# Half of a Fourier mix by a second level of Strassen's products: seven products of quarters over the hidden dimension, with the operands' split forms kept in DRAM

## The chip, the cores and the metric

The kernel runs on one core of a Trainium2 chip. The metric is the device time of one execution in microseconds. Several executions of the kernel before were timed, and one more was profiled; all numbers of a trace come from that one.

## The reference, cut to what matters

Two blocks are computed from the same `x` (2048 rows by 576 columns, float32) and mixed by a gate of one number per row:

```python
g = sigmoid((x * gate_w).sum(-1, keepdims=True))
a = linear_attention(x, wqkv, wo)            # 32 heads of 18, phi(t) = elu(t) + 1 + 1e-6
re = einsum("bsd,ed->bse", x, dft_hid_re)    # over the hidden dimension D = 576
im = einsum("bsd,ed->bse", x, dft_hid_im)
b = einsum("ts,bse->bte", dft_seq_re, re) - einsum("ts,bse->bte", dft_seq_im, im)   # over S = 2048
out = g * a + (1 - g) * b
```

The DFT matrices are ordinary inputs; the kernel multiplies by them as by any matrix.

## The kernel before, in words

Precision comes from splitting: each float32 operand is held as a rounded part ("hi", type fp32r, written by ScalarE in `hi_of`, L112) and a remainder ("lo", hi subtracted by VectorE in `lo_of`, L115). A product is hi·hi + hi·lo + lo·hi, three matmuls for each 128 rows of the contraction. Over D = 576 = 4·128 + 64 that is 4·3 + 2 = 14 matmuls for a result tile of 128 rows and 288 columns (half of the output's columns): the last 64 rows of hi and lo share one block of 128 rows. `steps` lists these 14, `run` (L123) issues them.

The program goes through seven stages, and TensorE's instructions stand in this order:

1. K: 16 tiles of 128 rows of `x` times `wk`, features by ScalarE and VectorE (`k_half`).
2. G: `x` transposed times K's features (L408), then the products with `wv` and `wo` that make a 576x576 matrix M per head group.
3. Q and M: 16 tiles of `x` times `wq` (`q_tile`), their normalisation on VectorE (`normalise`), a transpose on TensorE (`transposed`, L719) and the product with M. Row tile `i` of the result stands in SBUF as `acc[i]`.
4. First "pairs" stage (`pairs`): the hidden product with `dft_hid_re`. It goes over 8 pairs of row tiles (p and p + 8), each pair 2 tiles by 2 halves of 14 matmuls, 56 in all; from the four results `columns` and `rest` make seven combinations of 128x288, split in hi and lo (tile `f`).
5. First "sequence" stage (`sequence`, L663): the product with `dft_seq_re` as seven products of quarters (Winograd's form of Strassen's scheme), 8 groups j of 4 batches of 42 matmuls. `Matrix` loads the batches (`craw`, 512 KB each), VectorE adds, ScalarE and VectorE split. At a group's end VectorE adds seven banks of PSUM to four quarters and mixes them into `acc` by the gate (L679).
6. and 7. The same two stages with `dft_hid_im` and `dft_seq_im`; the last mix goes to the output.

The `x` tiles of the pairs stages are loaded from DRAM raw (`xraw`, 320 KB, L174) and split anew in each of the two stages, and `wr`/`wi` likewise (`Wide`, L225, L226). SBUF is laid out by hand: seven slots of 7168 bytes a partition serve the batches, and `LAY_R`/`LAY_I` say which places in them serve `x` tiles in the pairs stages. Queue SP issues nearly all DMAs; its order is written order up to the end of stage 3 (`manual_schedule`), and a planner's from there on. VectorE's, ScalarE's and TensorE's order is the planner's everywhere: it orders by simulated times when the program is built. GpSimd (POOL) does a few constants at the start.

Of the kernel before, what the change touches and what calls it, by code (L numbers as in the profile page):

```python
# [26 lines left out]
EPS = 1e-6  # L27

# [19 lines left out]
class Ring:  # L48
# [5 lines left out]
    def next(self):  # L54
# [18 lines left out]
LAY_R = dict(xs=(-256, 4864, 15744), hi=(20864, 9984), lo=(26624, 31232),  # L73
             low=(5, 3, 2, 1), high=(6, 0, 4))
LAY_I = dict(xs=(35840, 40960, 20096), hi=(25216, 14336), lo=(31232, 46080),
             low=(0, 4, 2, 3), high=(1, 5, 6))
# [3 lines left out]
def kernel(  # L80
# [7 lines left out]
    wo: bass.AP,  # L88
    wr: bass.AP,
    wi: bass.AP,  # L90
    cr: bass.AP,
# [14 lines left out]
    psum = ctx.enter_context(tc.tile_pool(name="psum", bufs=8, space=bass.MemoryType.PSUM))  # L106

# [5 lines left out]

    def lo_of(dst, src, hi):
        nc.vector.tensor_tensor(out=dst, in0=src, in1=hi, op=ALU.subtract)  # L115

    def add(dst, a, b, op=ALU.add):
        nc.vector.tensor_tensor(out=dst, in0=a, in1=b, op=op)  # L118

# [9 lines left out]
    in_order = ExitStack()  # L129
    in_order.enter_context(tc.manual_schedule(engines={mybir.EngineType.SP}))  # L130
# [46 lines left out]
    def split_next():  # L177
# [27 lines left out]
    class Wide:  # L205
# [22 lines left out]
        def split(self, h, n=1, keep=lambda ins: ins):  # L228
# [11 lines left out]
            keep(hi_of(hi[:, KC], rest))  # L240
# [19 lines left out]

    K_AT = T_AT + NT * XD
    pk = [at(T_AT + s * XD, [P, 2, D], R, "pk") for s in range(NT)]
    x_at(LAY_Q)
    wkt = Wide(wk, dict(hi=(0, WH), lo=(2 * WH, 2 * WH + WL)), K_AT)

    def k_half(i, h, xs):
        ps = bank()[:, :HALF]
        run(ps, steps(xs, lambda j: wkt.row(h, j)))
        feature(acc[i][:, half(h)], ps)
        if h == 1:  # L270
            hi_of(pk[i][:, 0], acc[i], EPS)
            nc.vector.scalar_tensor_tensor(pk[i][:, 1], acc[i], EPS, pk[i][:, 0],
                                           op0=ALU.add, op1=ALU.subtract)
# [32 lines left out]
    for h in range(2):  # L306
        for i in range(2):
            k_half(i, h, xs[i])
            if h == 1:
                load_next()  # L310
                if i == 0:
                    split_next()
# [17 lines left out]
    def xg_next():  # L330
        if xg_raw:
            c, t, raw = xg_raw.pop(0)
            hi_of(t[:, 0], raw)
# [5 lines left out]

    for i in range(2, NT):  # L340
        xs = split.pop(0)
        split_next()
        for h in range(2):
            k_half(i, h, xs)
        if i == NT - 2:
            for _ in range(4):
                xg_load()
        load_next()
    xg_next()
    xg_next()  # L350


    wqt = Wide(wq, LAY_Q, widths=QH)
    wq_splits = (s for h in range(2) for s in wqt.split(h, 2))
# [15 lines left out]
    def load_pair(o, src, n=P):  # L370
# [4 lines left out]
        hi_of(t[:n, 0], raw[:n])  # L375
        lo_of(t[:n, 1], raw[:n], t[:n, 0])
        return t
# [19 lines left out]
    wvt[0] = load_pair(wv_ring.next(), wv[:, 0])  # L397
    step = 0
    for c in range(5):
        ps = [bank(), bank()]  # L400
        passes = FULL if c < KC else FULL[:2]
        for q in range(NCU):
            t = xg_split.pop(0)
            for k in range(CU):
                s = q * CU + k
                for n, (a, b) in enumerate(passes):
                    for h in range(2):
                        nc.tensor.matmul(ps[h][:, :HALF], t[:, a, k], pk[s][:, b, half(h)],  # L408
                                         start=(s == 0 and n == 0),
                                         stop=(s == NT - 1 and n == len(passes) - 1))  # L410
            xg_load()
            xg_next()
            if q == 1 and c:
                kv_step(c - 1)
            if q == 2 and c < 4:
                wvt[c + 1] = load_pair(wv_ring.next(), wv[:, c + 1])
# [4 lines left out]
            elif step == NT - 1:  # L421
                z_chain()
            else:
                g = step - NT
                wot.append(load_pair(wo_at[g], wo[g * GW:g * GW + gsize(g)], gsize(g)))
            if step in (4, 5):
                wqt.load(step - 4)
            if step >= 8:
# [3 lines left out]
        for h in range(2):  # L432
            hi_of(gt[:, 0, half(h)], ps[h][:, :HALF])
            lo_of(gt[:, 1, half(h)], ps[h][:, :HALF], gt[:, 0, half(h)])
    split_next()
    wot.append(load_pair(wo_at[4], wo[4 * GW:], gsize(4)))


    def q_tile(i):
# [6 lines left out]
        nc.scalar.activation(g, ps[:, HALF:HALF + 1], AF.Exp, scale=-1.0)  # L446
# [69 lines left out]
    def split_m():  # L516
        for h in range(2):
            tc.keep_in_program_order(hi_of(mhi[:, :KC, half(h)], mraw[:, :, half(h)]))
# [7 lines left out]
    LEAD = 10  # L526
    q_tile(0)
# [5 lines left out]
    for i in range(3, LEAD):  # L533
# [3 lines left out]
        if i in (4, 6, 8):  # L537
            normalise(i // 2 - 2)
# [4 lines left out]
    factors = []  # L543

    def pairs(wd, m):


        def product(b, i, h, xs):
            run(b[i][h], steps(xs[i], lambda j: wd.row(h, j)))

        def banks():
            b12, b11, b22, b21 = (bank()[:, :HALF] for _ in range(4))
            return (b11, b12), (b21, b22)

        def columns(p, b):

            t = at(T_AT + p * TPAIR, [P, 2, 7, HALF], R, "f")
            for i in range(2):
                hi_of(t[:, 0, i], b[i][0])
                lo_of(t[:, 1, i], b[i][0], t[:, 0, i])  # L560
            return t

        def rest(b, t):
            (b11, b12), (b21, b22) = b
            s = at(Y_AT, [P, 4, HALF], F, "tsum")
            nc.scalar.activation(s[:, 3], b12, AF.Copy)
            add(s[:, 0], s[:, 3], b11, ALU.subtract)
            add(s[:, 2], b22, s[:, 3], ALU.subtract)
            hi_of(t[:, 0, 2], b22)
            add(s[:, 1], b22, s[:, 0], ALU.subtract)  # L570
            add(s[:, 3], s[:, 1], b21, ALU.subtract)
            lo_of(t[:, 1, 2], b22, t[:, 0, 2])
            hi_of(t[:, 0, 3:7], s)
            lo_of(t[:, 1, 3:7], s, t[:, 0, 3:7])
            factors.append(t)

        for p in range(NP - 2):
            xs = [split.pop(0), split.pop(0)]
            b = banks()
            for i, h in sorted(((0, 0), (0, 1), (1, 0), (1, 1)), key=lambda u: u[not p]):  # L580
                product(b, i, h, xs)
                if h == 1:
                    load_next()
                    split_next()
            rest(b, columns(p, b))
            if p == NP - 4:
                m.load(0)
                m.make(0)
        xs_ring.at, xs_ring.n = [T_AT + NP * TPAIR - XS], 0
        load_next()  # L590
        split_next()
        last, p = [], NP - 2
        for k in range(2):
            xs, b = [split.pop(0), split.pop(0)], banks()
            for i in (0, 1) if k == 0 else (1, 0):
                product(b, i, 0, xs)
            if k == 0:
                split_next()
            last.append((b, xs, columns(p + k, b)))
        m.load(1)  # L600
        for b, xs, t in last:
            for i in range(2):
                product(b, i, 1, xs)
            if t is last[0][2]:
                m.make(1)
            rest(b, t)


    class Matrix:


        def __init__(self, src, lay):
# [3 lines left out]
            self.low, self.high = Ring(0, 0, 0), Ring(0, 0, 0)  # L616
            self.low.at = [SLOT_AT + k * SLOT for k in lay["low"]]
            self.high.at = [SLOT_AT + k * SLOT for k in lay["high"]]

        def load(self, upto):  # L620
            while self.todo and self.loaded <= upto:
                j, b = self.todo.pop(0)
                o = self.low.next()
# [5 lines left out]
        def make(self, upto):  # L629
            while self.raws and self.made <= upto:  # L630
                r, o = self.raws.pop(0)
                add(r[:, 0:2], r[:, 4:6], r[:, 3].unsqueeze(1).to_broadcast([P, 2, BS, P]))
                add(r[:, 2], r[:, 1], r[:, 4])
                add(r[:, 3], r[:, 2], r[:, 6])
                hi = at(self.high.next(), [P, 7, BS, P], R, "c")
                lo = at(o, [P, 7, BS, P], R, "c")
                hi_of(hi, r)
                lo_of(lo, r, hi)
                self.ready.append((hi, lo))
                self.made += 1  # L640


    PRODUCTS = {1: (4, 0), 6: (2, 4), 2: (6, 1), 5: (1, 3), 7: (0, 5), 3: (3, 2), 4: (5, 6)}

    def sequence(m, g, last=None, between=None):
        late, held = [], []
        for n in range(NP * NB):
            j, b = divmod(n, NB)
            if b == 0:
                ps = {k: bank()[:, :HALF] for k in PRODUCTS}  # L650
            c = m.ready.pop(0)
            m.load(n + 3)
            m.make(n + 2)
# [4 lines left out]
            for q, (l, f) in PRODUCTS.items():  # L658
                for b, c in held:
                    for k in range(BS):  # L660
                        p = b * BS + k
                        for i, (x, y) in enumerate(FULL):
                            nc.tensor.matmul(ps[q], c[x][:, l, k], factors[p][:, y, f],  # L663
# [9 lines left out]
            y = at(Y_AT, [P, 2, 2, HALF], F, "y")  # L673
            c11, c12, c21, c22 = (y[:, i // 2, i % 2] for i in range(4))

            def mix(t, v, h=None, g=g, out=out if last is not None else None):
                a, cs = acc[t], slice(0, D) if h is None else half(h)
                a = a[:, cs]
                nc.vector.scalar_tensor_tensor(a, v, g[:, t:t + 1], a, op0=ALU.mult, op1=ALU.add)  # L679
                if out is not None:  # L680
                    nc.sync.dma_start(out=out[t * P:(t + 1) * P, cs], in_=a)
# [3 lines left out]
            add(c11, ps[2], c11)  # L685
            if end:
# [5 lines left out]
                mix(j + NP, c21, 0, out=None)  # L692
                mix(j, c12, 1, last, out=None)
                mix(j, ps[3], 1)
                mix(j + NP, ps[4], 0, last)
            else:
# [5 lines left out]
                late += [lambda t=t, i=i, y=y: mix(t, y[:, i].rearrange("p a b -> p (a b)"))  # L702
# [139 lines left out]
```

## Time and profile before

| | |
|---|---|
| time, median of 3 runs | 745.35 us (744.57 to 745.51) |
| the profiled execution: its own time, its span | 745.01 us, 743.3 us |
| TensorE busy | 735.4 us (99%), 5540 matmuls |
| VectorE busy, ScalarE busy | 543.2 us (73%), 331.9 us (45%) |
| GpSimd busy | 1.6 us |
| granted TensorE clock | full speed in all 40 slices |
| DMA | 75.55 MB, mean 102 GB/s |

The span is the profiled part of the execution; 1.7 us of the execution's time lie around it. "Busy" of TensorE counts pipelined matmuls end to end, so 99% says that matmuls followed each other without a gap, and not that the array did all it could. The DMA share in the views below is the mean busy share of the core's 16 DMA engines.

### The profile page before, as it was taken

Reading aid. Unit: us, or ns where it says so; the run is one execution under the profiler, and the core shown is the slowest. Engines: PE = TensorE matmul, PEld = TensorE weight load, DVE = VectorE, ACT = ScalarE, POOL = GpSimd, SP = SyncE. Lnnn points to the kernel's source line nnn. Section 1 sums busy time; section 2 is a strip of 40 time slices with the busy share of each in tenths; the row PEclk is TensorE's granted clock in tenths of the full one; section 3 lists DMA queues with packets and bytes.
Section 4 is the critical chain, followed back from the end, with each engine's and each line's share of the span. In section 5 each row is a group of like instructions: output and inputs, shape, how many; then the busy total and the mean of one; then the engine's idle time right before and its main releaser. Section 6 shows DMA issues by size and latency. Waiting matters only on the chain.

```text
span 743.3 us, 13515 instructions
## 1 busy us (share of the span) xinstructions
PE 735.4 (99%) x5540; PEld 734.1 (99%) x5540; DVE 543.2 (73%) x917; ACT 331.9 (45%) x536; POOL 1.6 (0%) x10
## 2 busy tenths in 40 slices
PE   7999999999999999999999999999999999999998
PEld 7999999999999999999999999999999999999998
DVE  5667843779957247788878778768778888777794
ACT  6777343767546335543332332334554333233321
POOL 0000000000000000000000000000000000000000
PEclk9999999999999999999999999999999999999999
DMA  5335535152112023223322322333323243334330
GB/s 168 90 90 158 179 106 145 54 169 72 36 59 92 1 82 89 72 86 115 114 86 88 112 86 86 114 118 117 90 77 113 67 159 130 117 125 139 117 118 33
DMA packets 31715, 75.55 MB, mean 102 GB/s; under 512 B 3301, under 2 KB 9061, under 8 KB 31653
## 3 DMA queue, kind: packets, MB, share of 16 engines
q1 hardware_dynamic: 31364, 74.27, 31.4%
q8 instruction: 44, 0.72, 0.4%
q10 hardware_dynamic: 288, 0.41, 0.2%
q14 instruction: 19, 0.15, 0.1%
HBM read 68.47 MB, written 4.72 MB: 98 GB/s over the span
## 4 chain that ended last, share of the span: by engine, by line
PE 99%; DMA 0%; DVE 0%; issue 0%; ACTq 0%; ACT 0%; DVEq 0%
PE bank L663 48%; PE bank L123 41%; PE bank L408 8%; PE bank L719 1%; DMA xraw<-in_xa_dram 0%; PE bank L391 0%; PE bank L394 0%; DVE acc L679 0%; DVE wd L115 0%; DVE xs L285 0%; ACTq L225 0%; ACT L147 0%; DVEq L115 0%; DVE xs L115 0%
## 5 line engine op out<-in xcount | busy, mean ns | idle before, releaser
L663 PE MATMUL bank<-f,c 128*128 128x288 f32 x2688 | 356.9, 295 | 0.0
L663 PEld LDWEIGHTS bank<-f,c 128*128 128x128 f32 x2688 | 356.6, 188 | 0.1
L123 PE MATMUL bank<-wd,xs 128*128 128x288 f32 (+1 forms) x1792 | 243.7, 297 | 4.5 <-DVE xs L115 3.8
L123 PEld LDWEIGHTS bank<-wd,xs 128*128 128x128 f32 x1792 | 240.7, 190 | 5.4 <-ACT wd L112 4.4
L112 ACT ACTIVATE c<-craw 128x1792 fp32r<-128x1792 f32 (+1 forms) x84 | 121.3, 1448 | 225.2 <-DVE craw L118 184.4
L115 DVE TENSOR_TENSOR c<-craw,c 128x1792 fp32r<-128x1792 f32 (+2 forms) x84 | 141.7, 1690 | 37.9 <-ACT c L112 37.7
L118 DVE TENSOR_TENSOR craw<-craw 128x256 f32<-128x256 f32 (+1 forms) x192 | 96.4, 509 | 50.4 <-DMA craw<-in_cr_dram 24.7
L115 DVE TENSOR_TENSOR xs<-xraw,xs 128x640 fp32r<-128x640 f32 (+1 forms) x65 | 52.5, 809 | 17.0 <-ACT xs L112 16.7
L123 PE MATMUL bank<-mw,qs 128*128 128x288 f32 x448 | 63.3, 297 | 0.0
L408 PE MATMUL bank<-pk,c 128*128 128x288 f32 x448 | 60.9, 296 | 0.0
L123 PEld LDWEIGHTS bank<-mw,qs 128*128 128x128 f32 x448 | 60.0, 188 | 0.0
L112 ACT ACTIVATE xs<-xraw 128x640 fp32r<-128x640 f32 x63 | 46.3, 737 | 30.4 <-DMA xraw<-in_xa_dram 30.1
L408 PEld LDWEIGHTS bank<-pk,c 128*128 128x128 f32 x448 | 59.8, 188 | 0.0
L118 DVE TENSOR_TENSOR y<-bank,y 128x288 f32<-128x288 f32 x63 | 28.6, 454 | 10.0 <-PE bank L663 9.3
L258 DVE SCALAR_TENSOR_TENSOR acc<-bank,e 128x288 f32<-128x288 f32 x64 | 27.8, 450 | 10.8 <-ACT e L257 10.7
L256 ACT ACTIVATE e<-bank 128x288 f32<-128x288 f32 x64 | 25.6, 401 | 19.2 <-PE bank L123 19.2
L115 DVE TENSOR_TENSOR f<-tsum,f 128x1152 fp32r<-128x1152 f32 x16 | 21.7, 1356 | 13.3 <-ACT f L112 13.3
L257 ACT ACTIVATE e<-e 128x288 f32<-128x288 f32 x64 | 28.0, 439 | 1.0
L112 ACT ACTIVATE f<-bank 128x288 fp32r<-128x288 f32 x48 | 19.2, 402 | 19.6 <-PE bank L123 11.0
L738 ACT ACTIVATE acc<-bank,gate 128x288 f32<-128x288 f32 x32 | 16.0, 500 | 26.4 <-PE bank L123 26.2
L115 DVE TENSOR_TENSOR f<-bank,f 128x288 fp32r<-128x288 f32 x48 | 21.4, 448 | 8.6 <-ACT f L112 8.6
L112 ACT ACTIVATE f<-tsum 128x1152 fp32r<-128x1152 f32 x16 | 18.6, 1162 | 17.3 <-DVE tsum L118 17.3
(69 smaller groups left out, 329.2 us busy)
## 6 DMA issues: line engine op xcount, KB each, us to landing
xraw<-in_xa_dram SPq DMA_DIRECT2D x63, 320.0 KB
craw<-in_cr_dram SPq DMA_DIRECT2D x32, 512.0 KB
craw<-in_ci_dram SPq DMA_DIRECT2D x32, 512.0 KB
craw<-in_xg_dram SPq DMA_DIRECT2D x20, 256.0 KB
out_dram<-acc SPq DMA_DIRECT2D x14, 288.0 KB
wraw<-in_wv_dram SPq DMA_DIRECT2D x5, 288.0 KB
wraw<-in_wr_dram SPq DMA_DIRECT2D x2, 576.0 KB
wraw<-in_wi_dram SPq DMA_DIRECT2D x2, 576.0 KB
```

What stands on the lines that cost most here:

```text
L112: return nc.scalar.activation(dst, src, AF.Copy, bias=bias)
L115: nc.vector.tensor_tensor(out=dst, in0=src, in1=hi, op=ALU.subtract)
L118: nc.vector.tensor_tensor(out=dst, in0=a, in1=b, op=op)
L123: nc.tensor.matmul(ps, a, b, start=(n == 0), stop=(n == len(pairs) - 1))
L256: nc.scalar.activation(e, ps, AF.Relu, scale=-1.0)
L257: nc.scalar.activation(e, e, AF.Exp, scale=-1.0)
L258: nc.vector.scalar_tensor_tensor(dst, ps, 0.0, e, op0=ALU.max, op1=ALU.add)
L408: nc.tensor.matmul(ps[h][:, :HALF], t[:, a, k], pk[s][:, b, half(h)], start=(s == 0 and n == 0), stop=(s == NT - 1 and n == len(passes) - 1))
L663: nc.tensor.matmul(ps[q], c[x][:, l, k], factors[p][:, y, f], start=(p == 0 and i == 0), stop=(p == NP - 1 and i == 2))
L719: nc.tensor.transpose(banks[c // KC][:, (c % KC) * P:(c % KC + 1) * P], a, ident)
L738: nc.scalar.activation(acc[i][:, half(h)], ps[:, :HALF], AF.Copy, scale=gate[:, i:i + 1])
```

## The change

**Products over D.** The hidden product of a pair is itself taken as one step of Strassen's scheme: the pair's `x` is cut into quarters (row tile p or p + 8, first or second half of D), `w` too, and seven products of quarter forms replace the eight quarter products that 56 matmuls made. A quarter contraction has 288 = 2·128 + 32 rows: 2·3 matmuls, and one more in which the three products of the last 32 rows stand under each other as 96 rows. So a product is 7 matmuls and a pair 49. `Hidden.run` writes the seven products of a pair in the order `ORDER`, two of them added in PSUM onto an earlier one (`start=False` at products 6 and 1), and what were `columns` and `rest` become seven additions of VectorE for each pair that go straight into the raw form of `f` and are split there (`Factors`).

**Split forms through DRAM.** The seven forms of `x` of each pair (`Left`) and of `wr`/`wi` (`right`) are made once, during stages 1 to 3 (for `wi` during stage 5), and written in split form to scratch tensors in DRAM: `xm` 1.84 MB a pair, `xr` 344 KB a pair (the last 32 rows), `wm` 4.9 MB a transform. GpSimd's queue issues these loads and stores. The pairs stages read them back on SP: `load_x` four chunks a pair (`xf`, three of 524 KB and one of 262 KB), `load_rest` (`xr`), `load_w` 590 + 111 KB a product (`wf`). Pairs 0 and 1 of the first transform are used where they were made. The raw `x` tiles of the pairs stages fall away.

**Room.** `acc` no longer stays in SBUF: the attention result goes out to a scratch tensor `att` tile by tile on GpSimd's queue, is read back as `row` in the first sequence stage, stored as `mid`, and read back in the second, whose mix is stored to `out`.

**Order.** VectorE's and ScalarE's instructions stand in written order in stages 1 (from tile 2), 2 and 4 to 7 (`pace`), TensorE's in 4 to 7, SP's everywhere. `lo_later` and `tick` put a subtraction behind the next piece of ScalarE's work; `make` of a batch is a generator that is advanced at written places.

The diff's core (the host's new layouts, the address tables and the K and G stages' edits are left out):

```diff
+    class Left:
+        def __init__(self, k, start, after):
...
+            for i in range(2):
+                begin_after(nc.gpsimd.dma_start(out=self.f[:, 4 * i + 1:4 * i + 3, 1],
+                                                in_=xq[k, :, 2 * i:2 * i + 2]), after)
+        def make(self):
+            r, c = self.f[:, :, 1], self.c
+            add(r[:, 0], r[:, 1], r[:, 6])
+            add(r[:, 4], r[:, 2], r[:, 6], ALU.subtract)
+            yield
+            add(r[:, 3], r[:, 0], r[:, 2], ALU.subtract)
+            add(r[:, 6], r[:, 5], r[:, 3], ALU.subtract)
+            yield
+            hi_of(c[:, :4, 0], r[:, :4])
+            yield
+            hi_of(c[:, 4:, 0], r[:, 4:])
+            lo_of(c[:, :4, 1], r[:, :4], c[:, :4, 0])
+            yield
+            lo_of(c[:, 4:, 1], r[:, 4:], c[:, 4:, 0])
+            if self.k < NP:
+                nc.gpsimd.dma_start(out=xforms[self.k], in_=c.bitcast(F))
...
-        for p in range(NP - 2):
-            xs = [split.pop(0), split.pop(0)]
-            b = banks()
-            for i, h in sorted(((0, 0), (0, 1), (1, 0), (1, 1)), key=lambda u: u[not p]):
-                product(b, i, h, xs)
...
+        def product(self, ps, p, k, start):
+            x, (w, wl) = self.x[p, k], self.w[k]
+            ops = [(x[:, a, c * P:c * P + P], w[:, 2 * c + b]) for c in range(2) for a, b in FULL]
+            ops.append((self.rest[p][:96, 6 - k], wl[:96]))
...
+        def run(self, m):
+            for p in range(NP):
...
+                for k, q in enumerate(ORDER):
+                    ps = {3: be, 6: be, 2: bx, 1: bx, 7: bg, 5: bg, 4: bf}[q]
+                    self.product(ps, p, k, q in (3, 2, 7, 4, 5))
+                    if p + 2 < NP and p not in self.taken and k in (1, 3, 5, 6):
+                        self.load_x(p + 2, k // 2 * 2)
+                    if p == 1 and k == 3:
+                        m.load(0)
...
+                for k in range(0, 7 if p in self.taken else 0, 2):
+                    self.load_x(p + 2, k)
+                if p + 2 < NP:
+                    self.load_rest(p + 2)
...
     def late(n):
...
+        if n == NP * NB - 2:
+            second.load_x(0, 0)
+            second.load_x(0, 2)
+            second.load_w(4)
+        if n == NP * NB - 1:
+            second.load_w(5)
+            second.load_w(6)
+            for k in (2, 4, 6):
+                second.load_x(1, k)
```

TensorE, first pairs stage: one product before (row tile p, half h; `wd` are the parts of `wr`, `xs` an `x` tile).

```order
L123 MATMUL bank_3330<-wd_321_2870,xs_329_2882 128x288
L123 MATMUL bank_3330<-wd_322_2871,xs_329_2882 128x288
L123 MATMUL bank_3330<-wd_321_2870,xs_329_2882 128x288 x2
L123 MATMUL bank_3330<-wd_322_2871,xs_329_2882 128x288
L123 MATMUL bank_3330<-wd_321_2870,xs_329_2882 128x288 x2
L123 MATMUL bank_3330<-wd_322_2871,xs_329_2882 128x288
L123 MATMUL bank_3330<-wd_321_2870,xs_329_2882 128x288 x2
L123 MATMUL bank_3330<-wd_322_2871,xs_329_2882 128x288
L123 MATMUL bank_3330<-wd_321_2870,xs_329_2882 128x288 x3
```

And now the start of pair 2 in the same stage (`xf` are its chunks, `xr_442` its last 32 rows, used by every product's seventh matmul):

```order
L799 MATMUL bank_3725<-wf_384_3214,xf_438_3619 128x288 x6
L799 MATMUL bank_3725<-wf_385_3215,xr_442_3627 128x288
L799 MATMUL bank_3726<-wf_392_3280,xf_438_3619 128x288 x6
L799 MATMUL bank_3726<-wf_393_3281,xr_442_3627 128x288
L799 MATMUL bank_3727<-wf_404_3432,xf_439_3621 128x288 x6
L799 MATMUL bank_3727<-wf_405_3433,xr_442_3627 128x288
L799 MATMUL bank_3725<-wf_409_3517,xf_439_3621 128x288 x6
```

A product went from 14 matmuls to 7, and pair 2's first product already needs `xr_442`.

Queue SP, from the first sequence stage's end into the second pairs stage, before:

```order
L174 DMA xraw_512_5684<-in_xa_dram 128x640
L225 DMA wraw_509_5679<-in_wi_dram 128x4x288
L174 DMA xraw_520_5738<-in_xa_dram 128x640
L174 DMA xraw_514_5729<-in_xa_dram 128x640
L225 DMA wraw_517_5733<-in_wi_dram 128x4x288
L625 DMA craw_552_6230<-in_ci_dram 128x1024
L174 DMA xraw_562_6325<-in_xa_dram 128x640
```

And now, from the last weights (`wf_665`) on, with the `xf` of pairs 1 and 2 (`xm_25`, `xm_26`):

```order
L772 DMA wf_665_6093<-wm_428_3541 128x1152
L773 DMA wf_666_6094<-wm_429_3542 96x288
L785 DMA xf_667_6097<-xm_25_95 128x1024
L785 DMA xf_668_6099<-xm_25_95 128x1024
L785 DMA xf_669_6101<-xm_25_95 128x512
L967 DMA mid_419_3532<-row_648_5880 128x576
L967 DMA mid_427_3540<-row_649_5881 128x576
L785 DMA xf_679_6143<-xm_26_96 128x1024
L785 DMA xf_680_6161<-xm_26_96 128x1024
L785 DMA xf_681_6181<-xm_26_96 128x1024
L785 DMA xf_682_6193<-xm_26_96 128x512
L778 DMA xr_683_6198<-xr_32_102 96x896
```

Pair 2's last block `xr_683` stands behind all of this, and two stores that wait for VectorE's mix stand ahead of pair 2's chunks.

Queue GpSimd (POOL) ends before with its constants:

```order
masks.py:199 AFFINE_SELECT ident_1_60<-ident_1_60 128x128
L150 AFFINE_SELECT mask_4_69<-mask_4_69 126x126
L152 AFFINE_SELECT mask_4_69<-mask_4_69 126x126
L838 UNCONDITIONAL_BRANCH
L838 ISA
```

And now it issues 60 DMAs; these stand at the end of stage 3 (`att_305` is the last attention tile):

```order
L355 DMA xm_24_94<-xb_363_3027 128x3584
L1032 DMA att_299_2338<-acc_17_87 128x576
L355 DMA xm_25_95<-xb_365_3031 128x3584
L1032 DMA att_300_2339<-acc_18_88 128x576
L1032 DMA att_301_2340<-acc_19_89 128x576
L1032 DMA att_302_2341<-acc_20_90 128x576
L1032 DMA att_303_2342<-acc_21_91 128x576
L1032 DMA att_304_2343<-acc_22_92 128x576
L1032 DMA att_305_2344<-acc_23_93 128x576
```

The room of the last two `acc` tiles takes pair 1's `xr` block in the first pairs stage, so that load waits for `att_305`.

More of the change, by code (lines that the diff above doesn't have):

```diff
@@ L536 @@
             move_m(g)
-        if i in (4, 6, 8):
-            normalise(i // 2 - 2)
+        if i in (6, 8):
+            normalise(i // 2 - 3)
+        next(wr_pieces)
         if i == LEAD - 2:
             split_m()
[L543 to L575, printed above, removed]
-        for p in range(NP - 2):
-            xs = [split.pop(0), split.pop(0)]
-            b = banks()
-            for i, h in sorted(((0, 0), (0, 1), (1, 0), (1, 1)), key=lambda u: u[not p]):
-                product(b, i, h, xs)
[L582 to L606, printed above, removed]
@@ L685, in sequence @@
             add(c11, ps[2], c11)
+            next(new, None)
             if end:
@@ L724, in transposed @@
         return xs
-    wdr = Wide(wr, LAY_R)
+    att = [scratch([P, D], "att") for _ in range(NT)]
+    hidden = Hidden(wr_forms, Layout(0))
     qs = transposed(0)
```

506 lines of the change are left out of this document (393 added, 113 removed).

## The prediction

> **What bounds the kernel now.** I read the page's busy times first, then the chain of waits in order of time, TensorE's own waits, and the windows by stage.
>
> ```profile
> span 743.3 us, 13515 instructions
> ...
> PE 735.4 (99%) x5540; PEld 734.1 (99%) x5540; DVE 543.2 (73%) x917; ACT 331.9 (45%) x536; POOL 1.6 (0%) x10
> ...
> PEclk9999999999999999999999999999999999999999
> ```
> ```profile
> 6.39 61.05 PE bank L123 x444
> ...
> 186.35 0.55 PE bank L719 x5
> ...
> 257.17 66.78 PE bank L123 x504
> 323.95 178.43 PE bank L663 x1344
> 502.38 59.34 PE bank L123 x448
> 561.72 178.21 PE bank L663 x1344
> 739.95 0.52 DVE acc L679
> ```
> ```profile
> PE bank L123 <- DVE xs L115: 3.8, 1, 3.8
> PE bank L123 <- DVE wd L115: 0.4, 1, 0.4
> PE bank L123 <- DVE xs L285: 0.2, 1, 0.2
> ```
>
> From 6.39 us to 740.5 the chain is TensorE alone, at the full granted clock; it waited 4.4 us in three waits, all while the first operands arrived. So time can be won only by taking matmuls away, and every microsecond that TensorE is made to wait is lost in full. The second pairs stage holds nothing but its 448 matmuls: 59.34 / 448 = 132.5 ns each, or 7.42 us a pair.
>
> **The matmuls taken away.** A pair goes from 56 to 49, 8 pairs, twice: 112 fewer. The seventh matmul of a product has 96 rows instead of 128; rows of this trace say whether that matters:
>
> ```profile
> L123 PE MATMUL bank<-wd,xs 128*128 128x288 f32 x1568 | 215.0, 297 | 4.5 <-DVE xs L115 3.8 <-DVE wd L115 0.4 <-DVE xs L285 0.2
> L123 PE MATMUL bank<-plain,kvb 72*72 72x288 f32 x6 | 1.1, 296 | 0.0
> ```
>
> 72 rows took 296 ns, 128 took 297: the columns set the time. So the term is -112 x 0.1325 = **-14.8 us**, and a pair takes 6.49 us, a product 0.93. Nothing else is taken from TensorE (5428 matmuls stay), so no better time than this is to be had; the question is how much waiting comes back.
>
> **What the loads add.** The pairs stage read two 320 KB tiles a pair. Now it reads 2.18 MB (seven forms of 128 x 512 floats, 1.84 MB, and the last rows, 0.34 MB) in 6.49 us: 336 GB/s.
>
> ```profile
> 257.20:323.95 66.75, 66.75 (x506) 66.75 (x506) 42.20 (x78) 31.92 (x56) 0.00 (x0) 1.00 0.26 76
> 502.38:561.72 59.34, 59.34 (x450) 59.34 (x450) 45.77 (x83) 30.12 (x52) 0.00 (x0) 1.00 0.31 95
> 561.72:740.50 178.78, 178.19 (x1344) 177.96 (x1343) 140.85 (x202) 57.31 (x43) 0.00 (x0) 1.00 0.33 112
> ```
> ```profile
> 401.94 0.33 SPq L625 DMA_DIRECT2D craw<-in_cr_dram  x1
> ```
> ```profile
> 402.75:403.00 0.25, 0.25 (x4) 0.25 (x3) 0.25 (x1) 0.00 (x0) 0.00 (x0) 1.00 0.04 16
> 403.75:404.00 0.25, 0.25 (x5) 0.25 (x3) 0.25 (x1) 0.00 (x0) 0.00 (x0) 1.00 1.04 410
> 404.00:404.25 0.25, 0.25 (x4) 0.25 (x3) 0.14 (x1) 0.00 (x0) 0.00 (x0) 1.00 0.98 393
> 404.50:404.75 0.25, 0.25 (x4) 0.25 (x3) 0.00 (x0) 0.25 (x1) 0.00 (x0) 1.00 0.45 180
> ```
> ```profile
> 405.31 0.69 DVE L118 TENSOR_TENSOR craw<-craw 128x512 f32<-128x512 f32 x1 [1.17 <-DMA craw<-in_cr_dram]
> ```
>
> The last two columns of a window are the DMA engines' busy share and GB/s. The stage has run at 76 to 95 GB/s, so the new rate was never tried; one 512 KB batch shows the parts. Issued at 401.94, first bytes at about 403.0 (1.1 us), at full share 393 to 410 GB/s, last bytes at about 404.7, VectorE starts 0.6 later. Its rows are 4 KB each, as the new chunks' are, so of the rates I take the nearest, 390 GB/s. The low end is 112 / 0.33 = 340, what the sequence stage's rate gives at full share, starts of transfers included.
>
> *Second transform.* At its start T the last batch's slots come free, and SP has queued, in order: two products' weights (1.40 MB), three chunks of pair 1 (1.31), two stores of `mid` (0.59), pair 2's chunks (1.83), pair 2's last rows (0.34): 5.48 MB. At 390 these last rows land at T + 1.3 (0.2 to the issue, 1.1 to first bytes) + 14.05 + 0.6 = 16.0. Pair 2's seventh matmul wants them at 2 x 6.49 + 0.8 = 13.8: a wait of 2.2 us. The next pair has 2.70 MB ahead of it (a batch of 0.52 MB stands among them): 22.9 against 22.5, 0.4 us more. From then on 2.18 MB take 5.6 us of a pair's 6.49, and the queue catches up. Together 2.6 us; at 340 the same steps give 4.2 + 1.5 = 5.7.
>
> *First transform.* Pairs 0 and 1 are there already, but all of pair 2 is issued only when pair 0's products are done, at T + 6.5: landed at 14.0 against 13.8 (0.2), and pair 3, behind a batch, 0.4 late. Together 0.6 us; at 340 it is 1.0 + 1.4 = 2.4.
>
> The term is **+3.2 us**, between 0 (the queue reaches 410 and more, or starts sooner) and 8.1. [...]
>
> **VectorE and ScalarE.** In the pairs stage a pair now has seven additions and one subtraction of 288 columns and two of 864:
>
> ```profile
> L118 DVE TENSOR_TENSOR tsum<-bank,tsum 128x288 f32<-128x288 f32 x32 | 14.4, 449 | 0.4 <-PE bank L123 0.4
> L115 DVE TENSOR_TENSOR f<-tsum,f 128x1152 fp32r<-128x1152 f32 x16 | 21.7, 1356 | 13.3 <-ACT f L112 13.3
> L112 ACT ACTIVATE f<-bank 128x288 fp32r<-128x288 f32 x48 | 19.2, 402 | 19.6 <-PE bank L123 11.0
> L112 ACT ACTIVATE f<-tsum 128x1152 fp32r<-128x1152 f32 x16 | 18.6, 1162 | 17.3 <-DVE tsum L118 17.3
> ```
>
> The 864-column piece lies between: 1.05 us (ScalarE 0.91). VectorE: 8 x 0.45 + 2 x 1.05 = 5.7 of 6.49 us; ScalarE 3 x 0.40 + 2 x 0.91 = 3.0. TensorE adds product 5 onto a bank that VectorE must have read: after the copy of product 2 (done at 2.5 us into the pair), ScalarE's 0.91 and VectorE's 1.05, that read ends at about 4.9, and product 5 starts at 5.56: 0.7 us to spare, and 0.2 in pairs 3 and 4, where a batch's addition stands in between. Cost 0; if VectorE is late there, up to 0.2 us a pair, 3 in all.
>
> The forms of `x` and `w` are now made earlier. One `Left` is four additions of 256 columns and subtractions of 1024 and 768, one `right` piece four of 288 and 2016: each about 4 us of VectorE.
>
> ```profile
> 6.39:67.44 61.05, 61.05 (x446) 60.93 (x447) 39.37 (x68) 46.04 (x98) 0.00 (x0) 1.00 0.38 116
> 67.44:127.00 59.56, 59.56 (x457) 59.56 (x456) 36.27 (x61) 25.35 (x49) 0.00 (x0) 1.00 0.46 140
> 136.00:168.00 32.00, 32.00 (x244) 32.00 (x243) 27.00 (x67) 22.18 (x62) 0.00 (x0) 1.00 0.46 131
> 168.00:192.00 24.00, 24.00 (x185) 24.00 (x184) 24.00 (x54) 16.06 (x39) 0.00 (x0) 1.00 0.23 67
> 323.95:502.38 178.43, 178.43 (x1347) 178.29 (x1346) 142.27 (x202) 62.07 (x50) 0.00 (x0) 1.00 0.31 101
> ```
> ```profile
> 184.02 0.27 DVE L115 TENSOR_TENSOR qs<-bank,qs 128x128 fp32r<-128x128 f32 x1
> ```
>
> VectorE is busy 39 of 61 us in K, 36 of 60 in G and 142 of 178 in the sequence: three forms more in each leave it under 90%, and the cover is gone only past that. The narrow place is 136 to 192, where it has 5 us idle and then none. Up to the second `qs` split some 5 us of work come in (pieces of `wr` for two `normalise` that move later), and four splits of `wo`, 3 us, move out ahead of it. That split ended at 184.3, its matmuls began after the transposes of 186.35: 2.6 us to spare, and 5 idle before. Cost 0, at most 3. In the sequence, `att`, `mid` and `row` add 9.4 MB to 178 us: 101 to 154 GB/s, hidden at a share of 0.5.
>
> **GpSimd's queue.** No DMA of GpSimd is in this trace. 26 of them stand from the first `att` store (after the first product with M, which ends a few us ahead of the transposes of 186.35, about 183) to the last, which must land before pair 1's last rows are loaded; TensorE wants those at 257.2 + 6.5 + 0.8 = 264.5. Less a store and a load (some 3 us each, the batch above took 3.4), 75 us for 26: up to 2.9 us each costs nothing. The nearest price is SP's 0.33 us an issue, so I take 0; dearer, it costs 26 us for each microsecond above 2.9.
>
> ```profile
> L715 DVE COPY twice<-acc 128x128 f32<-128x128 f32 x16 | 3.4, 220 | 12.6 <-PE bank L719 12.6
> ```
>
> [...]
>
> **The sum.** 745.0 (the profiled execution's time; its span is 743.3) - 14.8 + 3.2 + 0 = 733.4. The median of the runs is 0.3 above that execution; I say **733.6 us**.
>
> **Rivals.** *Nothing waits* (0.18): the queue starts sooner or runs at 410, and the 14.8 us stand: 730.2 to 731.5. For it speaks that TensorE waited nowhere after the start; against it, that the loads of pair 2 have 5.5 MB ahead of them. *The loads bound the pairs stages* (0.18): at 340 or below, 8 us and more come back, at 310 a pair alone takes 7.0 us: 737 to 743. For it, the sequence's 340; against it, the 393 to 410 inside one transfer. *GpSimd's queue bounds stage 3* (0.09): the other side. If one of its DMAs takes over 3.4 us, the 11.6 us are gone; at 4.0 the last `att` store is 28 us late and the time 761. [...] *The change doesn't do what it says*: TensorE's order holds 5428 matmuls, so this is out.
>
> **How the numbers follow.** The likeliest case, a wait of 2 to 6 us, has 0.52 and 733.6. Within 0.2% of before (743.9 to 746.8), about what a measurement here can tell from no change, 0.03. The range 730.1 to 740.0 takes in the floor, the likeliest case and two thirds of the slow loads: 0.82. Faster: 0.52 + 0.18 + 0.18 = 0.88; same 0.03; slower 0.09.
>
> **What would show it.** In the profile after: 5428 matmuls; TensorE's waits, few, at pair 2 and 3 of each pairs stage, on `xr`, longer in the second; DMA share near 1 there, and GB/s the rate to put for 390. If waits stand at `acc` or `wf` at the end of stage 3, it was GpSimd's queue; waits for `fl` or a bank in every pair mean VectorE is the bound. A shorter span than 728.4, or a pair unlike 6.49 us where nothing waits, would break the first term.

## The result, and the profile after

The changed kernel takes 797.58 us (median of 4 runs, 795.73 to 799.38), the kernel before 745.43 (744.57 to 745.86): ratio 1.0701, 95% interval 1.0675 to 1.0727. It is 7% slower; 733.6 was predicted, in a range up to 740.

From the page of the kernel after: the span, the busy times, TensorE's granted clock in 40 slices, and the chain that ended last by engine; then that last line for the kernel before.

```profile
span 797.7 us, 13789 instructions
...
PE 737.6 (92%) x5428; PEld 729.8 (91%) x5428; DVE 594.4 (75%) x993; ACT 334.6 (42%) x518; POOL 41.0 (5%) x70
...
PEclk9999998599899999999999999989899999999999
...
PE 69%; DMA 15%; DVE 7%; SPq 4%; issue 2%; ACT 2%; DVEq 0%; ACTq 0%
```
```profile
PE 99%; DMA 0%; DVE 0%; issue 0%; ACTq 0%; ACT 0%; DVEq 0%
```

The 5428 matmuls are there. But the chain, 99% TensorE before, is now 69%: TensorE idles 797.7 - 737.6 = 60.1 us (7.9 before). And 112 matmuls fewer, 14.8 us, should have brought its busy time from 735.4 to 720.6; it is 737.6. The clock row has a 5 and four 8s where all was 9: for part of the time TensorE ran at a lower clock (more on this at the end).

TensorE's waits in the kernel after (what it waited for: us in all, times, the longest):

```profile
PE bank L581 <- DVE c L168: 26.7, 2, 25.9
PE bank L799 <- DMA xr<-xr: 9.8, 7, 4.3
PE bank L949 <- DVE c L168: 5.8, 5, 3.4
PE bank L188 <- DVE xs L168: 3.9, 1, 3.9
PE bank L188 <- ACT kvb L158: 3.7, 2, 2.8
...
PE bank L799 <- DMA wf<-wm: 0.3, 1, 0.3
```

One wait of 25.9 us stands in the G stage (L581), where the prediction looked for nothing. The 3.9 us at the start were there before. For the last rows of `x` (`xr`) TensorE waited 9.8 us in seven waits: 2.3 and 1.2 us at pairs 2 and 3 of the first stage, 4.3 at pair 2 of the second, and four of 0.3 to 0.9 at later pairs. For weights (`wf`), which would have pointed to GpSimd's queue, it waited 0.3.

By stage, from the first start of one stage's matmuls to the first start of the next one's (us; the other columns are the main experiments below):

| stage | before | after | e1 | e5 | e9 | e12 |
|---|---|---|---|---|---|---|
| G and Q/M | 197.1 | 238.4 | 209.0 | 208.9 | 208.3 | 202.2 |
| pairs, first | 59.4 | 58.6 | 57.0 | 53.7 | 53.1 | 54.5 |
| sequence, first | 178.4 | 187.9 | 188.7 | 185.3 | 182.0 | 183.0 |
| pairs, second | 59.3 | 61.9 | 61.1 | 55.9 | 55.0 | 55.5 |
| sequence, second | 178.1 | 179.9 | 178.4 | 179.1 | 179.7 | 179.2 |

So 41 us are lost in G and Q/M, 10 in the first sequence, and the pairs stages, which should win 7.4 us each, win 0.8 and lose 2.6.

SP's queue around the long wait (start, length, line, what: a load of `wv`, the six stores, a load of `x` rows), the six stores by themselves (shortest, median and longest issue in ns, first and last start), and the window 135 to 140 us (busy us of PE, PEld, DVE, ACT, POOL; then the clock, the DMA engines' share and GB/s):

```profile
118.32 0.33 SPq L543 DMA_DIRECT2D wraw<-in_wv_dram  x1
118.81 26.93 SPq L359 DMA_DIRECT2D xr<-xb  x6
145.84 5.21 SPq L484 DMA_DIRECT2D craw<-in_xg_dram  x1
```
```profile
L359 SPq DMA_DIRECT2D xr<-xb x6: 685/5123/5431, 118.8 to 140.5; - x6
135.00:140.00 5.00, 0.00 (x0) 0.00 (x0) 0.00 (x0) 0.00 (x0) 0.00 (x0) 0.50 0.29 87
```

Six stores (L359) put the last rows' forms into `xrest`. Issuing one takes SP 5.1 us at the median, where the load of `wv` ahead of them took 0.33. The load of `x` rows that the G stage needs stands behind them and is itself held for 5.2 us; in the window TensorE, VectorE, ScalarE and GpSimd stand still. The DMA engines are at a share of 0.29: little more than a quarter is in use.

### The profile page after: what moved, and what is told of

The parts are those of the page before. It is cut to its first block, busy times and chain, and to the rows that moved or that the text cites. A ratio compares the mean times of both kernels' runs of the same rounds, so it can differ in the third digit from the quotient of the medians.

```text
span 797.7 us, 13789 instructions
## 1 busy us (share of the span) xinstructions
PE 737.6 (92%) x5428; PEld 729.8 (91%) x5428; DVE 594.4 (75%) x993; ACT 334.6 (42%) x518; POOL 41.0 (5%) x70
## 4 chain that ended last, share of the span: by engine, by line
PE 69%; DMA 15%; DVE 7%; SPq 4%; issue 2%; ACT 2%; DVEq 0%; ACTq 0%
PE bank L949 37%; PE bank L188 20%; PE bank L799 8%; DMA xr<-xr 5%; SPq L359 3%; DMA craw<-in_xg_dram 2%; PE bank L581 2%; DVE c L168 2%; DMA xraw<-in_xa_dram 2%; DMA craw<-in_cr_dram 2%; PE bank L1010 1%; DVE craw L178 1%; DMA xf<-xm 1%; DMA craw<-in_ci_dram 1%; DMA xm<-xb 1%
## 5 line engine op out<-in xcount | busy, mean ns | idle before, releaser
L949 PE MATMUL bank<-fh,c 128*128 128x288 f32 x1792 | 361.2, 297 | 5.8 <-DVE c L168 5.8
L949 PEld LDWEIGHTS bank<-fh,c 128*128 128x128 f32 x1792 | 289.4, 189 | 7.9 <-DVE c L168 7.4
L949 PE MATMUL bank<-fl,c 128*128 128x288 f32 x896 | 265.6, 296 | 0.0
L949 PEld LDWEIGHTS bank<-fl,c 128*128 128x128 f32 x896 | 170.1, 190 | 0.0
L168 DVE TENSOR_TENSOR c<-craw,c 128x1792 fp32r<-128x1792 f32 (+4 forms) x86 | 141.9, 1652 | 27.6 <-ACT c L158 27.5
L188 PE MATMUL bank<-wd,xs 128*128 128x288 f32 (+1 forms) x896 | 126.9, 303 | 7.6 <-DVE xs L168 3.9
L188 PEld LDWEIGHTS bank<-wd,xs 128*128 128x128 f32 x896 | 123.9, 194 | 8.9 <-ACT wd L158 4.5
L799 PE MATMUL bank<-wf,xf 128*128 128x288 f32 x588 | 93.8, 300 | 0.9 <-DMA xf<-xm 0.5
L581 PE MATMUL bank<-pk,c 128*128 128x288 f32 x448 | 63.5, 302 | 28.5 <-DVE c L168 26.7
L581 PEld LDWEIGHTS bank<-pk,c 128*128 128x128 f32 x448 | 61.5, 193 | 29.3 <-DVE c L168 27.0
L799 PEld LDWEIGHTS bank<-wf,xf 128*128 128x128 f32 x588 | 85.6, 193 | 1.6 <-DMA xf<-xm 0.8
L799 PE MATMUL bank<-wf,xr 96*128 96x288 f32 x112 | 34.9, 311 | 9.9 <-DMA xr<-xr 9.8
```

Of the source, the lines that this page charges most:

```text
L188: nc.tensor.matmul(ps, a, b, start=(n == 0), stop=(n == len(pairs) - 1))
L799: nc.tensor.matmul(ps, a, b, start=(start and n == 0), stop=(n == len(ops) - 1), skip_group_check=True)
L949: nc.tensor.matmul(ps[q], c[x][:, l, k], factors[p](y, f), start=(p == 0 and i == 0), stop=(p == NP - 1 and i == 2))
```

## The experiments

**e1, e2: the six stores.** Theories: the stores run on few DMA engines (4 of 16 would be a share of 0.25, near the 0.29), which the author's theory puts down to the outermost dimension of their target, 4 blocks of 32 partitions; or SP pays for each of the 896 rows of 512 bytes.

```diff
-for j in range(6):
-    k, g = j // 2, j % 2
-    nc.sync.dma_start(out=xrest[g, :, k], in_=c[:, :, k // 2, g * P:g * P + P])
+for j in range(24):                                   # e1
+    p, k, g = j // 6, j // 2 % 3, j % 2
+    nc.gpsimd.dma_start(out=xrest[g, p, k], in_=c[32 * p:32 * p + 32, ...])
...
+for j in range(12):                                   # e2: stays on nc.sync
+    p, k, g = j // 6 * 2, j // 2 % 3, j % 2           # out=xrest[g, p:p + 2, k]
```

> The six stores of the last rows are cut into 24 (one for each block of 32 partitions) and put on GpSimd's queue, which is empty there; nothing else changes. If SP's six issues of 5.2 us are what kept the row loads of the G stage back, TensorE's wait of 25.9 us and the 1.7 us at half clock behind it go: about 797.6 - 27.6 = 770 us, with the other waits (3.7 and 3.0 us at the start of the Q stage, 3.4 near the end of the first sequence, 9.8 on xr) still there. If the late operands there are only a sign of something else (the DMA engines full, VectorE late), the wait moves and the time stays above 785.

> The six stores stay on SP, but each is cut in two, so that its outermost dimension is 2 blocks instead of 4: twelve stores of half the bytes and half the rows. Theory 'few engines' (a store runs on as many DMA engines as its outermost dimension divides into, 4 before, 2 now, and holds SP until those have taken its rows): 224 rows for each engine as before, so 5.2 us an issue as before, 12 x 5.2 = 62 us, DMA share 0.14 while they run, and the kernel at about 797.6 + 31 = 829 us. Theory 'rows' (SP pays for each of the 896 rows of 512 bytes, however spread): 2.6 us an issue, 31 us in all, and the kernel within 3 us of 797.6.

e1: 767.27 us, 30.3 less than after (ratio to before 1.0294, interval 1.0268 to 1.032). e2: 826.69 in one execution. In e2, the stores and a window while they run:

```profile
L359 SPq DMA_DIRECT2D xr<-xb x12: 667/5203/5682, 120.4 to 174.0; - x12
135.00:140.00 5.00, 0.00 (x0) 0.00 (x0) 0.00 (x0) 0.00 (x0) 0.00 (x0) 0.53 0.14 41
```

Half the rows and half the bytes a store, and the same 5.2 us, where theory 'rows' had 2.6; the share is halved too, 0.29 to 0.14. So between these two kernels the price goes neither by a store's rows nor by its bytes. It agrees with theory 'few engines': with 4 and 2 of 16 at work the share would be 0.25 and 0.13, and each engine would have 224 rows of 512 bytes in both. A store's bytes at the measured rate (459 KB at 87 GB/s, 229 KB at 41) take an estimated 5.3 and 5.6 us, about as long as its issue, and the six held SP for 26.9 us. On how many engines a store runs no trace shows, and that the outermost dimension sets it was the author's theory, tried with 4 and 2 blocks alone. e1 cuts the stores finer and moves them to another queue at once; what each of the two is worth by itself was not measured.

**e3, e4, on e1: the written order, and the loads of the last rows.** e3 takes VectorE and ScalarE out of the written order; e4 loads no `xr` after pair 1.

> The run with the stores cut into 24 on GpSimd's queue, and besides VectorE and ScalarE no longer in written order: the scheduler orders them. If the written order is what makes the operands late at the start of the Q stage and near the end of the first sequence (3.7, 3.0 and 3.4 us of waits, with half clock behind them 16 us in all), this is 5 to 16 us faster than that run. If the order is harmless and loads come late, within 3 us of it; if the scheduler's order is worse, slower by more.

> The run with the stores cut into 24 on GpSimd's queue, and besides pairs 2 to 7 load no last rows of their own and use those of pairs 0 and 1 (12 loads of 344 KB left out, their rows are wrong). If the DMA engines' rate bounds the pairs stages, 0.34 of 2.18 MB a pair are gone, a pair's 1.84 MB take 4.7 us at 390 GB/s against 6.5 of matmuls, and the waits go: 58.6 and 61.9 us become about 53 each, 13 to 15 us less than that run. If the loads only start late (their places come free late), the waits pass on to xf and no more than 5 us are won.

e3: 768.10 in one execution, e1's time: taken as a whole, the written order is not what costs. e4: 752.62 in one execution, 14.7 less, with pairs stages of 52.2 and 53.8 us: in the first, where nearly nothing is late, the 49 matmuls do take 6.5 us a pair. But e4 took away bytes and lateness together.

**e5, on e1: the same bytes in another order.** Each pair's last rows come in four parts, each behind the chunk of the same forms.

```diff
 self.load_x(p + 2, k // 2 * 2)
+self.rest_part(p + 2, k // 2 * 2)
 ...
-if p + 2 < NP:
-    self.load_rest(p + 2)
```

> The run with the stores cut into 24 on GpSimd's queue, and besides the last rows of a pair come in four parts, each issued right behind the chunk of the same forms, instead of as one load behind all four chunks; the bytes are the same. Theory 'rate' (2.18 MB a pair are more than the DMA engines move in 6.5 us): the waits pass from xr to xf or stay, and no more than 3 us are won on 767.3. Theory 'order' (the last rows are issued last, at the end of pair p - 2, and wanted first, by the first product of pair p: at most 7.3 us for a queue of 2.2 MB): the 7.9 us of waits on xr and most of the half clock behind them go, 8 to 13 us faster, near 756.

756.58 us, 10.7 less than e1 (1.0147, 1.0126 to 1.0168). First the chain of the kernel after in the first pairs stage (start, length, what), then e5's remaining waits for the two kinds of load:

```profile
320.43 9.26 DMA xr<-xr
329.73 6.00 PE bank L799 x43
...
336.02 7.71 DMA xr<-xr
343.77 6.80 PE bank L799 x49
350.57 7.55 DMA xr<-xr
```
```profile
PE bank L806 <- DMA xf<-xm: 2.1, 3, 1.0
PE bank L806 <- DMA xr<-xr: 0.2, 1, 0.2
```

Each load of `xr` is issued when a pair ends, behind four chunks of the same later pair, and the three here land 7.6 to 9.3 us after their issue; TensorE wants it 7.3 us after (a pair and a product). Of the six such loads TensorE waited for five in the first stage and for two in the second. With the same bytes in another order 10.7 us are gone, so the order was the larger part.

The rate is not out of it, though. Windows inside the first pairs stage of the kernel after, of e5, and of e4 without the last rows (the last two columns are the DMA engines' share and GB/s):

```profile
314.00:354.00 40.00, 35.82 (x262) 34.64 (x260) 30.77 (x57) 17.71 (x28) 0.00 (x0) 1.00 1.03 331
```
```profile
287.00:325.00 38.00, 37.70 (x282) 37.37 (x282) 33.16 (x63) 17.14 (x28) 0.00 (x0) 1.00 1.04 339
```
```profile
288.00:325.00 37.00, 37.00 (x280) 37.00 (x280) 32.85 (x63) 16.95 (x28) 0.00 (x0) 1.00 0.87 302
```

At a full share the DMA engines moved 331 and 339 GB/s, and a pair's 2.18 MB in 6.49 us want 336. In order the loads just fit, with nothing to spare: e5's pairs stages, 53.7 and 55.9 us, are still 3.6 us longer together than e4's. What holds the rate there below the 393 to 410 GB/s inside one batch's transfer was not looked into.

**e6, on e1: the burst of weights.** One product's weights in each of batches 23 to 26 instead of four in batch 26; `rest(1)` at batch 5, the pieces of `wi` two batches earlier.

```diff
-if n == 26:
-    for k in range(4):
-        second.load_w(k)
-    second.load_rest(1)
+if 23 <= n <= 26:
+    second.load_w((3, 0, 1, 2)[n - 23])
+if n == 5:
+    second.load_rest(1)
```

> The run with the stores cut into 24 on GpSimd's queue, and besides the weights of the second transform are loaded one product a batch (batches 23 to 26) and not four at batch 26, rest(1) at batch 5, and the pieces of wi are made two batches earlier. If the 4.7 us of TensorE's wait at 498 us come from the batch that is loaded behind 3.1 MB issued within 7 us, that wait and the 1.9 us at half clock behind it go: 5 to 7 us faster, near 761. If VectorE's order makes the batch late, the wait stays and the time is within 2 us of 767.3.

761.19 us, 6.1 less than e1 (1.0208, 1.0193 to 1.0224). In e1, the first load of the burst on SP and the batch's load behind it, and VectorE's additions that wait for a load of the same kind; then e6's waits of TensorE in the sequences:

```profile
482.48 0.32 SPq L772 DMA_DIRECT2D wf<-wm  x1
...
489.26 0.37 SPq L890 DMA_DIRECT2D craw<-in_cr_dram  x1
```
```profile
499.88 1.61 DVE L178 TENSOR_TENSOR craw<-craw 128x512 f32<-128x512 f32 x3 [5.46 <-DMA craw<-in_cr_dram]
```
```profile
PE bank L949 <- DVE c L168: 2.6, 3, 1.4
```

The three edits of e6 were not tried one by one.

**e7, e8: the G stage at 74 us and the start of the M stage.** e7, on e1, splits two x tiles of the Q stage later and lets GpSimd make the additions of `wr`'s pieces; e8 is e7 with the edits of e5 and e6.

> The run with the stores cut into 24 on GpSimd's queue, and besides: the split of two x tiles that only the Q stage needs stands three steps later in the G stage, so that ScalarE does not wait for their load ahead of the split that TensorE waits for (2.2 us of wait at 74 us and 1.7 at half clock); and the additions of the pieces of wr are made by GpSimd and not by VectorE, which is busy without a gap from 169 to 190 us, where TensorE waits 2.6, 0.7 and 0.6 us. If both places are as said, 6 to 8 us faster, near 760; if GpSimd makes its pieces so late that the weights are late at 276 us, or the two engines hinder each other, less, and slower than 767 is possible.

> The three edits together, on the run with the stores cut into 24: if each place is a cause of its own, their gains add to 19 to 28 us: 739 to 748 us, about the kernel before. If a wait that is taken away only lets the next one show, 750 or more.

e7: 768.52 (1.0305, 1.026 to 1.035), no gain; e8: 753.21 (1.0141, 1.0071 to 1.0211), no better than e5 and e6 together would be (750.5). Both guesses of e7 failed: the split in the way at 74 us was a third one, placed there by the scheduler, and GpSimd took 1.0 us for an addition that takes VectorE 0.45.

**e9: stores, order, weights and that third split mended. e10 to e14, on e9: what holds the start of the M stage.**

```diff
-if step in (1, 2):                    # e9
+if step in (1, 2, 5):
     split_next(lo_later)
 ...
-split_next()                          # e9, in q_tile
+if i:
+    split_next()
 ...
-next(wr_pieces)                       # e10: later, and what follows of them too
+if i < LEAD - 2:
+    next(wr_pieces)
...
+# e11: the subtraction of wr's pieces by nc.gpsimd.tensor_tensor
+# e12: without these subtractions
+# e13: wr's two loads after q tile 1 and at q tile 3; e14: e12 and e13
```

> The stores cut into 24 on GpSimd's queue, the last rows in order and the weights spread, all three, and besides the x tile whose split ScalarE has ahead of the splits that TensorE waits for at 74 us is split at step 5 of the G stage, in the written order, instead of wherever the scheduler puts it. Sum of the parts: 767.3 - 10.7 - 6.1 = 750.5, and 2.2 us of wait and up to 1.7 at half clock less at 74 us: 746.6. If that split was not the cause, 750.5.

> The run before, and besides the pieces of wr are not made at q tiles 8 and 9, and all that follows of them comes two steps later, into the M stage. If VectorE, busy without a gap from 169 to 190 us, is what TensorE waits for there (2.6 + 0.7 + 0.6 us), up to 4 us faster, near 743. If VectorE has no room in the M stage either, the waits come later and the time is the same or worse.

> The same without that delay, but GpSimd makes the subtraction that ends each piece of wr (2.3 us of VectorE for each of two pieces), which only the piece's store waits for. If VectorE's load from 169 to 190 us is the cause, up to 4 us faster than 746.6; if GpSimd's slower subtraction (its additions took 1.0 us for 288 columns, so some 14 us for the two pieces) holds up the stores so far that the weights come late, slower.

e9: 750.52 (1.0073, 1.0058 to 1.0088): the sum of e1, e5 and e6, and no more. The wait at 74 us is gone; 2.0 us came in at 187.5 instead. e10: 755.33 (1.0128, 1.0103 to 1.0154), worse. e11: 751.36 (1.0084, 1.0056 to 1.0111), the same. In e9, ScalarE, VectorE and TensorE around the first wait:

```profile
168.71 0.74 ACT L158 ACTIVATE xs<-xraw 128x640 fp32r<-128x640 f32 x1 [2.90 <-DMA xraw<-in_xa_dram]
173.19 0.73 ACT L158 ACTIVATE xs<-xraw 128x640 fp32r<-128x640 f32 x1
```
```profile
174.81 2.33 DVE L168 TENSOR_TENSOR wb<-wb 128x1152 fp32r<-128x1152 f32 x2
177.05 0.82 DVE L168 TENSOR_TENSOR xs<-xraw,xs 128x640 fp32r<-128x640 f32 x1
```

The x tile that TensorE waits for until 177.9 was split by ScalarE at 173.9; VectorE, without a gap since 169.5, subtracted 2.33 us of `wr` first. Two theories were left: VectorE's load, or the x tile's load, late by 2.9 us.

> The run with stores, last rows, weights and x tile mended, without VectorE's subtraction at the end of each piece of wr (two of 2.33 us and a small one; the low parts of wr's forms are left out). Theory 'VectorE': from 164 to 192 us it has no gap, the split that TensorE waits for at 176 us stands behind the first of these subtractions (174.81 to 177.05), and the wait at 187.5 behind the second: both go, with the half clock behind the second, 4 to 6 us faster, near 745.5. Theory 'load': the x tiles' loads come late (ScalarE waits 2.9 us for one at 165.8), everything behind is put off by it, and without the subtractions at most 1 to 2 us are won.

> The run with stores, last rows, weights and x tile mended, and besides the two loads of wr (0.58 MB each) are issued after q tile 1 and at q tile 3, some 8 us earlier each, when the DMA engines' share is 0.23, and not beside the x tiles' loads. Theory 'load': ScalarE's wait of 2.9 us for the x tile at 165.8 shrinks to 1 or less, TensorE's waits at 168 and 176 us (1.0 and 2.6) go, 3 to 5 us faster, near 747. Theory 'VectorE': its pieces only come a little earlier, the sum of its work is the same, within 1.5 us of 750.5.

> Both: the loads of wr earlier, and its low parts left out. If loads and VectorE each cause a part, this adds up to near 742; if one of them is the whole cause, it is at the better of the two.

e12: 746.76 us (1.0022, 1.0012 to 1.0032), 3.8 less than e9. e13: 749.72 (1.0066, 1.005 to 1.0083), 0.8 less, within the noise, as theory 'VectorE' had it. e14: 750.98 in one execution, not the better of the two but e9's time. TensorE after the transposes in e12 (its wait there is in brackets):

```profile
175.40 0.27 PE L1018 MATMUL bank<-ident,twice 128*128 128x128 f32 x1
176.05 7.19 PE L188 MATMUL bank<-wd,xs 128*128 128x288 f32 x52 [0.38 <-DVE xs L168]
183.55 3.95 PE L188 MATMUL bank<-mw,qs 128*128 128x288 f32 x28
```

The wait of 2.6 us is 0.4, that of 2.0 is gone. So in e9 VectorE's load holds this place. The loads are not free of blame: e13 lets its early loads meet other x tiles, and TensorE waits 3.5 us a few tiles ahead instead; in e14, without the subtractions, it waits 2.1 and 1.8 us for x tiles again. How the two share the cost is open. No version beat the kernel before: e9, which leaves nothing out, is 0.7% slower, and so is e13.

## Why the prediction was wrong, point by point

- **The matmuls taken away: right.** 5428 remain; with nearly nothing late (e4) a first pairs stage takes 52.2 us, and 8 x 6.49 = 51.9 was said.
- **The failed step: the stores of the last rows, never costed.** Under "VectorE and ScalarE" the forms made earlier were priced by their work on two engines; the DMAs that store the last rows, on the queue that feeds the G stage, were left out. In their place the runs showed six issues of 5.1 us that hold up the G stage's loads; with what TensorE lost behind them they are 30.3 of the 64.0 us that the forecast was off (e1). SP's 0.33 us an issue, which the prediction took for GpSimd's, does not hold on SP for these stores.
- **The loads: the right waits, the term mis-sized.** +3.2 us was said, 8.1 at most; the pairs stages of the kernel after stand 58.6 + 61.9 - 103.8 = 16.7 above their matmuls (16 x 6.49). 7.8 of the 9.8 us of waits on `xr` are at pairs 2 and 3, as said. The step that failed is "2.18 MB take 5.6 us of a pair's 6.49, and the queue catches up". That takes 390 GB/s; at a full share 331 were measured, so a pair's loads take 6.6 us and nothing is caught up. The prediction's steps at 331 GB/s give an estimated 9.2 us of waits, near the 9.8, though not at the same pairs (1.2, 1.7, 4.7 and 1.7 at pairs 2 and 3 of the two stages, against 2.3, 1.2, 4.3 and none). Half clock behind the wait of 4.3 took 2.2 us more; the other 4.7 of the 16.7 were not traced. And the steps took the order for given: the last rows are issued last and wanted first. With that mended (e5), at much the same rate, the term is 53.7 + 55.9 - 103.8 = 5.8. So the rival that the loads bound the stage had the place and the rate (340 or below); that another order of the same bytes takes most of it away, it did not have.
- **"Hidden at a share of 0.5", in the sequence: wrong by 6.1 us** (e6). The mean hid a burst: 3.1 MB issued from 482.5 to 489.2 us, and the batch issued then came 5.5 us late. The mean was off too: the stage moved 198 GB/s at a share of 0.58, not 154 at 0.5: the forms of `wi`, 4.9 MB stored and 4.9 MB loaded in it, were not counted.
- **VectorE, cost 0 and at most 3: the place was right, the size was not.** 136 to 192 us was named as the narrow place; in e9, with the stores, the order and the burst mended, `wr`'s subtractions there alone cost 3.8 us (e12).
- **GpSimd's queue: right.** An `att` store takes it 0.55 us in e1, 2.9 would have been free, and TensorE waited 0.3 us for weights.
- **The clock: not thought of.** "Every microsecond that TensorE is made to wait is lost in full" is too little: some 10 us were lost at half clock behind four waits, as shown below.

The terms found, 30.3 + 10.7 + 6.1 + 3.8, bring 797.6 to 746.7; e12, which leaves work out for the last of them, took 746.8. Of the 13 us that still part this from 733.6, e12's waits in the first sequence are 3.0 and its pairs stages stand 54.5 + 55.5 - 103.8 - 3.2 = 3.0 above the term; the rest is in G, Q/M and inside TensorE's busy time, where no wait names it, and stays open.

## What to carry to other kernels

Cost every DMA that a change adds on the queue that it is put on, stores too, and look at what stands behind it in that queue: one of the six stores took SP 5.1 us at the median, the load ahead of them 0.33. Compare the order in which loads are issued with the order in which they are wanted, and take the rate from a stretch as long as the stage: the 390 GB/s read off one transfer were 331 to 339 over 40 us. A mean share of 0.5 over a stage says nothing about a burst of 3 MB in 7 us inside it.

## What the runs showed of the hardware

**A wait of 2 to 4 us can cost more than itself.** Windows of the kernel after, three waits and the stretch behind each (columns as above; the clock is the third number from the end), and a wait of e9 with the stretch behind it:

```profile
318.00:322.00 4.00, 1.71 (x13) 1.48 (x12) 2.84 (x6) 0.93 (x1) 0.00 (x0) 1.00 1.03 293
323.00:327.00 4.00, 4.00 (x32) 4.00 (x31) 2.42 (x5) 1.64 (x3) 0.00 (x0) 1.00 1.05 365
201.00:205.30 4.30, 1.30 (x9) 0.82 (x7) 4.30 (x8) 3.46 (x8) 0.00 (x0) 0.88 0.57 156
206.00:210.00 4.00, 4.00 (x19) 3.98 (x19) 3.94 (x7) 3.37 (x6) 0.93 (x1) 0.50 0.60 228
529.00:533.00 4.00, 0.56 (x4) 0.32 (x4) 3.72 (x5) 1.70 (x1) 0.00 (x0) 0.87 0.17 68
534.00:538.00 4.00, 4.00 (x18) 4.00 (x18) 3.93 (x6) 1.70 (x1) 0.00 (x0) 0.50 0.70 234
```
```profile
186.00:190.00 4.00, 1.99 (x15) 1.75 (x14) 4.00 (x10) 2.75 (x8) 0.92 (x1) 1.00 0.66 224
190.00:193.40 3.40, 3.40 (x16) 3.40 (x15) 3.40 (x7) 1.33 (x5) 0.00 (x0) 0.50 1.01 386
```

In the kernel after, the clock stays full after 2.3 idle us of 4; after 3.0 of 4.3, and 3.4 of 4, TensorE comes back at half clock, 19 and 18 matmuls in 4 us against 32. But e9 shows half clock after 2.0 idle us of 4, so the length of the idle time alone does not decide it; what else does is not shown. In the kernel after it happens four times, and TensorE works at half clock for 3.5 to 6 us each: some 20 us, 10 us lost on top of the waits.

**GpSimd beside VectorE.** In e11, VectorE's subtraction of an x tile, 0.82 us in e9, while GpSimd subtracts too, and TensorE's wait for it:

```profile
173.66 4.86 POOL L372 TENSOR_TENSOR wb<-wb 128x1152 fp32r<-128x1152 f32 x2 [12.15 <-ACT wb L158]
```
```profile
176.67 2.52 DVE L168 TENSOR_TENSOR xs<-xraw,xs 128x640 fp32r<-128x640 f32 x1
```
```profile
179.25 2.11 PE L188 MATMUL bank<-wd,xs 128*128 128x288 f32 x9 [3.65 <-DVE xs L168]
```

2.52 us, and TensorE's wait behind it is 3.65 us where e9's was 2.6: at this place a subtraction on VectorE took three times as long while GpSimd had one under way. What made it slower is not shown, nor that this is why e11 won nothing: this execution, of 746.8 us, was the shortest of six with a median of 751.4, and where the others lost their time no trace tells.
